# Attention output products at slots 9, 11, 13 and 14 of a tile, and a last output split into 352 and 160 columns

## The chip, the cores and the metric

The kernel runs on one core of one Trainium2 chip. The metric is the device time of one execution in microseconds (us). Before the change it is 293.71 us, the median of 6 runs, which lie between 293.46 and 293.94 us. A core has a matrix engine (TensorE, PE in the profile, with its weight loads shown as PEld), VectorE (DVE), ScalarE (ACT) and GpSimd (POOL), and SyncE (SP), which here only issues transfers. Each engine works through its own queue in order, and engines wait for each other on semaphores. PSUM is the memory that the matrix engine writes its results to; other engines copy ("evict") the results from there.

## The reference

Inputs are q, k and v, each 8 batches x 8 heads x 576 positions x 64, and the weights of a feed-forward block. Everything is float32; the kernel computes the products in bfloat16.

```
q_s = softmax of q over its last axis (64);  k_s = softmax of k over the positions (576)
kv  = einsum('bhsd,bhse->bhde', k_s, v)          # 64 x 64 for each batch and head
att = einsum('bhsd,bhde->bhse', q_s, kv)
x   = att as 4608 tokens x 512
h   = x @ w_in                                    # 4608 x 2048
g   = h + sin(alpha * h)**2 / alpha
out = g @ w_out                                   # 4608 x 512
```

## The kernel before, in words

The 4608 tokens are cut into nine tiles of 512 (t = 0 to 8). A batch of the attention has 576 tokens, nine groups of 64, so tiles and batches do not line up: batch b fills the columns 576b to 576b + 575 of `xT`, the transposed attention result (4 x 128 features by 4608 tokens), and tile t reads the columns 512t to 512t + 511 of it.

A tile is a loop over 16 *slots* (`ni`), one for each 128 of the 2048 hidden features. In slot `ni` of tile t, `mm_h` (L226, matmuls at L235) makes one 128x512 block of h with four matmuls of 512 columns; `sine` (L239) runs Sin on ACT (L241) and then the square, on ACT (L243), POOL (L245) or DVE (L247); `combine` (L250, instruction at L251) makes the bfloat16 block of g on DVE. Each h block lies in one PSUM buffer until its combine has run. There are four such buffers, taken in turn; in tile 2 slots 4, 5, 10 and 11 borrow others.

The second product, g @ w_out, runs as a stream (`o_stream`, L408, matmuls at L255): for each of the four groups of 128 tokens of a tile, 16 matmuls of 512 columns accumulate in one PSUM bank, and `evac_o` (L258) copies the bank to SBUF (L261) and writes it out with two transfers (L264). From tile 3 on the stream of tile t-1 is woven into the slots of tile t: two or three of its matmuls follow each slot's `mm_h` (L488), after 23 of them in slot 0. The third group of 128 tokens ends in slot 10, and its copy, on DVE, stands behind combine(10) in DVE's queue.

The attention of a later batch is woven in too. In tiles 3 to 6 that is batch b = t + 1; in tile 2 it is batch 3. For tiles 3 to 6: in slot 0 ACT takes the exponentials of q and k, and DVE and POOL normalise q into `qn`; in slot 4 `q_transpose_dma` (L194) asks SP for a transposing transfer of `qn` into `qT`; and `attn_back` (L451), called in slot `ni` with n = `ni` - 5, does the rest. At n = 0 (slot 5) it makes the kv products and DVE normalises them into `kbd`. Then it calls `attn_out` (L206) four times. Call number m makes feature pair m // 2 and half m % 2 of the batch's tokens: half 0 is the first 256 tokens, half 1 the other 320. A call is two matmuls (L212) of 256 or 320 columns into the two banks of a PSUM tile `xp`, and one cast (L215) that evicts both into `xT`. I name the calls xp0 to xp3 and their casts xT0 to xT3. `xp` comes from the pool `ps_a`, which has one buffer: the matmuls of a call cannot start before the cast of the call before has ended. In tiles 3 to 6 all casts are on DVE; in tile 2 they alternate between two engines, taken by the parity of n.

The order of the code is the order of each queue. In tiles 3 to 6 a slot is: `mm_h(ni)`, `attn_back`, `sine(ni)`, `combine(ni)`, the stream. So a cast in slot `ni` stands on DVE between combine(ni-1) and combine(ni). In tile 2 (L463 to L466) a slot is: `mm_h(ni)`, `sine(ni)` with its square, `combine(ni-2)`, `attn_back`. So a cast of slot `ni` stands on ACT behind Sin(ni), and behind square(ni) where `SQ2` gives that square to ACT; on DVE it stands behind combine(ni-2). Slots 9, 11 and 14 of tile 2 have the square on ACT, slots 10, 12, 13 and 15 on POOL. There is no output stream in tile 2.

Tiles 7 and 8 carry no attention. After tile 8 (L493 to L499) the output stream of that tile runs alone. Three groups of 128 tokens go as before; the last group is made in two parts of 256 columns, each with 16 matmuls (L498), a copy on DVE and two transfers of 64 tokens, one issued by SP and one by ACT.

Of the kernel before, what the change touches and what calls it, by code (L numbers as in the profile page):

```python
# [15 lines left out]
F32 = mybir.dt.float32  # L16
# [7 lines left out]
def kernel(  # L24
# [14 lines left out]
    nc = tc.nc  # L39
    ctx.enter_context(nc.allow_non_contiguous_dma(reason="layout"))  # L40
    B, H, S, D = q.shape
    dm = H * D
# [4 lines left out]
    nN = d_ff // 128  # L47
    MF = 512
    nT = NT // MF
# [19 lines left out]
    wout = singles.tile([128, nN, dm], BF16, name="wout")  # L69
# [76 lines left out]
    def kv_mm(b, ii, pool, split=False):  # L146

        if ii == 0 or split:
            A["kvp", b] = pool.tile([128, 2, 512], F32, name="kvp", tag="a")
        kvp, ke, vt = A["kvp", b], A["ke", b], vb[b % 2]  # L150
        for j in range(J):
            for e in range(2):
                r = slice(64 * e, 64 * e + 64)
                nc.tensor.matmul(kvp[:, e, ii * 130:(ii + 1) * 130],  # L154
                                 ke[r, j, ii * 128:(ii + 1) * 128],
                                 vt[r, j, ii * 130:(ii + 1) * 130],
                                 start=(j == 0), stop=(j == J - 1))

    def kv_norm(b, i0=0, i1=2):

        kt, m = kbd[b % 2], i1 - i0
        kvr = small.tile([128, 2, 2, 2], F32, name="kvr")[:, :, 0:m]
        src = A["kvp", b][:, :, i0 * 130:i1 * 130].rearrange("p e (ii x c) -> p e ii x c", ii=m, x=2)
        nc.vector.reciprocal(kvr, src[:, :, :, :, D])
        for x in range(2):
            r = slice(64 * x, 64 * x + 64)
            nc.vector.tensor_tensor(kt[r, :, i0:i1, r], src[r, :, :, x, 0:D],
                                    kvr[r, :, :, x].unsqueeze(3).to_broadcast([64, 2, m, D]), op=ALU.mult)
# [37 lines left out]
    def attn_out(b, ii, half, pool, eng):  # L206
        qT, kt = A["qT", b], kbd[b % 2]
        j0, j1 = XO[half]
        n = (j1 - j0) * P
        xp = pool.tile([128, 2, 512], F32, name="xp", tag="a")  # L210
        for e in range(2):
            nc.tensor.matmul(xp[:, e, 0:n], kt[:, e, ii], qT[:, ii, j0:j1, e * 64:(e + 1) * 64],  # L212
                             start=True, stop=True)
        c0 = (J * b + j0) * P
        eng(xT[:, 2 * ii:2 * ii + 2, c0:c0 + n], xp[:, :, 0:n])  # L215
# [8 lines left out]
    G = {}  # L224
# [29 lines left out]
    def mm_o(t, j, ni, acc):  # L254
        nc.tensor.matmul(acc, G[t][:, ni, j * 128:(j + 1) * 128], wout[:, ni, :],  # L255
                         start=(ni == 0), stop=(ni == nN - 1))

    def evac_o(t, j, acc, eng, cols=None, queues=None):  # L258
        cols = cols or slice(0, dm)
        o = opool.tile([128, dm], F32, name="o")  # L260
        eng(o[:, cols], acc)  # L261
        for hf in range(2):
            blk = t * BPT + 2 * j + hf
            (queues or (nc.sync, nc.sync))[hf].dma_start(out=out_v[blk // J, blk % J][:, cols],  # L264
                                                         in_=o[64 * hf:64 * hf + 64, cols])


    ACT_CP, DVE_CP, GP_CP = nc.scalar.copy, nc.vector.tensor_copy, nc.gpsimd.tensor_copy
# [59 lines left out]
    def h_slot(t, ni, sq, lag, wide=None):  # L328
        hp = mm_h(t, ni, wide)
        lag.append((t, ni, hp, sine(t, ni, hp, sq)))  # L330

    def flush(lag, keep):
        while len(lag) > keep:
            combine(*lag.pop(0))
# [14 lines left out]
    def take(it, n=1000):  # L349
        for _ in range(n):  # L350
            if next(it, 0) == 0:
                return
# [4 lines left out]
    with tc.tile_pool(name="ps_e", bufs=2, space=PSUM, reuse_waits="tile") as ps_e:  # L357
# [4 lines left out]
        for ni in range(nN):  # L362
            h_slot(0, ni, "PAPDPAPADPAPPDAP"[ni], lag, lent)
            flush(lag, 1)
            if ni in late:
                name, x, b, hv = late[ni]
# [37 lines left out]
    ps_o = ctx.enter_context(tc.tile_pool(name="ps_o", bufs=2, space=PSUM, reuse_waits="tile"))  # L404
    ps_a = ctx.enter_context(tc.tile_pool(name="ps_a", bufs=1, space=PSUM, reuse_waits="tile"))


    def o_stream(t, eng=DVE_CP):  # L408
        for j in range(4):
            acc = ps_o.tile([128, dm], F32, name="op", tag="o")  # L410
            for ni in range(nN):
                mm_o(t, j, ni, acc)
                if ni == nN - 1:
                    evac_o(t, j, acc, eng)
                yield
# [20 lines left out]
    c0 = J * 2 * P  # L436
# [11 lines left out]
    q_transpose_dma(3)  # L448
    load_batch(4)

    def attn_back(b, n, engs=(DVE_CP, DVE_CP)):  # L451
        if n == 0:
            kv_mm(b, 0, ps_a)
            kv_mm(b, 1, ps_a)
            kv_norm(b)
        elif 5 <= n < 9:
            attn_out(b, (n - 5) // 2, (n - 5) % 2, ps_a, engs[n % 2])

    def lent():
        return ps_o.tile([128, MF], F32, name="op", tag="o")  # L460
# [2 lines left out]
    for ni in range(nN):  # L463
        h_slot(2, ni, SQ2[ni], lag, lent)
        flush(lag, 2)
        attn_back(3, ni - 5, (DVE_CP, ACT_CP))  # L466
    flush(lag, 0)

    for t in range(3, nT):
        b = t + 1 if t + 1 < B else None  # L470
        os = o_stream(t - 1)
        done = 0
        for ni in range(nN):
            hp = mm_h(t, ni)
            if b is not None:
                if ni == 4:
                    q_transpose_dma(b)
                attn_back(b, ni - 5)
            s = sine(t, ni, hp, "A")
            combine(t, ni, hp, s)  # L480
            if b is not None and ni == 0:
                exp_q(b)
                exp_k(b)
                cast_v(b, [GP_CP, GP_CP])
                norm_q(b, [GP])
                if b + 1 < B:
                    load_batch(b + 1)
            want = 23 + 21 * ni // 8 if b is not None else 4 * (ni + 1)  # L488
            take(os, min(64, want) - done)
            done = min(64, want)  # L490
        take(os)

    take(o_stream(nT - 1), 48)  # L493
    for h in range(2):
        cols = slice(h * 256, h * 256 + 256)
        acc = ps_o.tile([128, 256], F32, name="op", tag="o")
        for ni in range(nN):
            nc.tensor.matmul(acc, G[nT - 1][:, ni, 384:512], wout[:, ni, cols], start=(ni == 0), stop=(ni == nN - 1))  # L498
        evac_o(nT - 1, 3, acc, DVE_CP, cols, (nc.sync, nc.scalar))  # L499


# [1 line left out]
_INS = ['q', 'k', 'v', 'moe_w_in', 'moe_w_out', 'moe_alpha']  # L503
_OUTS = [((4608, 512), 'float32')]
# [25 lines left out]
```

The softmax here doesn't subtract the row's maximum and nothing guards it: scores larger than these inputs give would overflow.

## Time and profile before

| | |
|---|---|
| median of 6 runs | 293.71 us |
| the profiled execution: its own time | 293.54 us |
| its span, first to last instruction | 291.8 us |
| granted clock of TensorE | 1.000 |
| PE busy | 279.1 us (96%) |
| ACT busy | 226.9 us (78%) |
| DVE busy | 188.0 us (64%) |
| POOL busy | 85.4 us (29%) |
| chain that ended last, by engine | PE 76%, DVE 9%, ACT 5%, POOL 3%, issue 3%, DMA 3% |

How to read it: the busy time of PE is a sum of modelled matmul lengths that overlap, so 96% does not say that only 4% are idle. A matmul of 512 columns has a length of 379 ns in the records, but the next one starts 216 ns after it. The distance between starts is what counts: where a matmul starts later than that after the one before it, PE waited. In timeline lines the columns are the start and the length in us, the engine, the line, the operation with its output and inputs, the count of merged instructions, and in brackets the idle time ahead of it with what ended it.

### The profile page before, as it was taken

To read this page: it belongs to the slowest core of one execution; us is meant where nothing else is said; L and a number is where in the kernel's file an instruction comes from. 1 tells how busy PE (TensorE), PEld (TensorE's weight loads), DVE (VectorE), ACT (ScalarE), POOL (GpSimd) and SP (SyncE) were. 2 spreads that over 40 slices of the span, in tenths; PEclk is the share of its full clock that TensorE was granted. 3 is DMA by queue.
4 is the path that set the end of the run, shared out by engine and by line. 5 is a ranking of instruction groups with operands and counts; after the bars stand their busy time and mean duration, and the time that the engine had idled before them with its cause. 6 is when DMAs were issued, how large, how long until landed. Compare 5 with 4: busy or idle time off the path is not lost.

```text
span 291.8 us, 4261 instructions
## 1 busy us (share of the span) xinstructions
PE 279.1 (96%) x1576; PEld 132.6 (45%) x1576; DVE 188.0 (64%) x275; ACT 226.9 (78%) x320; POOL 85.4 (29%) x78
## 2 busy tenths in 40 slices
PE   2999999999999999999999999999999999999994
PEld 1444455444454445444444454444444444444444
DVE  3758955798958657864786568756774555555412
ACT  4779946999569899789987998799977777777500
POOL 0939581566674744002600061005000000000000
PEclk9999999999999999999999999999999999999999
DMA  7999999964889975109920993113411111111143
GB/s 245 308 180 206 356 254 333 396 230 124 209 144 368 393 241 117 37 19 335 293 49 19 289 316 72 36 39 67 86 38 36 36 36 38 36 36 37 38 108 73
DMA packets 35253, 45.77 MB, mean 157 GB/s; under 512 B 15888, under 2 KB 19744, under 8 KB 35232
## 3 DMA queue, kind: packets, MB, share of 16 engines
q1 hardware_dynamic: 29632, 34.09, 40.7%
q0 software_dynamic: 5408, 11.27, 15.2%
q8 instruction: 12, 0.20, 0.3%
q10 hardware_dynamic: 192, 0.14, 0.2%
q14 instruction: 9, 0.07, 0.1%
HBM read 36.71 MB, written 9.44 MB: 158 GB/s over the span
## 4 chain that ended last, share of the span: by engine, by line
PE 76%; DVE 9%; ACT 5%; POOL 3%; issue 3%; DMA 3%; ACTq 0%
PE op L255 32%; PE hp L235 31%; PE hp L255 4%; DVE g L251 3%; PE warm L299 2%; POOL s L245 2%; DVE xT L215 2%; ACT s L241 2%; PE xp L212 2%; PE kvp L154 2%; DVE o L261 1%; DMA st_q<-in_q_dram 1%; DMA qT<-qn 1%; PE op L498 1%; PE hh L235 1%
## 5 line engine op out<-in xcount | busy, mean ns | idle before, releaser
L251 DVE SCALAR_TENSOR_TENSOR g<-s,inva_sb,hp 128x512 bf16<-128x512 f32 x130 | 95.3, 746 | 64.6 <-ACT s L243 52.1
L235 PE MATMUL hp<-xT,win 128*128 128x512 bf16 x520 | 129.5, 379 | 0.2
L255 PE MATMUL op<-wout,g 128*128 128x512 bf16 x496 | 124.0, 379 | 0.0
L241 ACT ACTIVATE s<-hp,alpha_sb 128x512 f32<-128x512 f32 x130 | 87.8, 682 | 29.4 <-PE hp L235 25.3
L235 PEld LDWEIGHTS <-win 128*128 128x128 bf16 x576 | 56.1, 98 | 68.2 <-issue 2.0
L255 PEld LDWEIGHTS <-g 128*128 128x128 bf16 x560 | 54.1, 98 | 62.7 <-issue 1.6
L243 ACT ACTIVATE s<-s 128x512 f32<-128x512 f32 x112 | 70.6, 631 | 3.6
L143 POOL TENSOR_TENSOR qn<-qe,qs 128x1152 bf16<-128x1152 bf16 x13 | 27.5, 2129 | 83.8 <-DVE qs L137 67.7
L245 POOL TENSOR_TENSOR s<-s 128x512 f32<-128x512 f32 x27 | 28.4, 1059 | 24.0 <-ACT s L241 23.7
L261 DVE COPY o<-op 128x512 f32<-128x512 f32 (+1 forms) x33 | 21.9, 665 | 10.2 <-PE op L255 7.6
L114 ACT ACTIVATE qe<-st_q 128x1152 bf16<-128x1152 f32 x16 | 18.0, 1158 | 2.8 <-DMA st_q<-in_q_dram 2.8
L114 ACT ACTIVATE ke<-st_k 128x1152 bf16<-128x1152 f32 x16 | 17.8, 1152 | 3.0 <-DMA st_k<-in_k_dram 3.0
L136 DVE TENSOR_REDUCE qs<-qe 128x36 f32<-128x2304 bf16 x5 | 12.8, 2553 | 10.8 <-ACT qe L114 10.7
L128 POOL CAST vb<-st_v 128x1152 bf16<-128x1152 f32 x14 | 16.4, 1202 | 8.2 <-DMA st_v<-in_v_dram 8.2
L215 DVE CAST xT<-xp 128x512 bf16<-128x512 f32 (+1 forms) x22 | 16.5, 753 | 2.8 <-PE xp L212 2.7
L255 PE MATMUL hp<-wout,g 128*128 128x512 bf16 x64 | 15.1, 379 | 0.4 <-DVE g L251 0.3
L212 PE MATMUL xp<-qT,kbd 128*128 128x256 bf16 (+1 forms) x56 | 10.8, 285 | 2.1 <-DVE xT L215 1.0
L154 PE MATMUL kvp<-vb,ke 64*128 64x130 bf16 x288 | 9.8, 216 | 0.5 <-ACT qT L187 0.4
L114 ACT ACT_TABLE_LOAD x7 | 9.0, 1283 | 1.3 <-PEq L514 1.2
L154 PEld LDWEIGHTS <-ke 64*128 64x128 bf16 x288 | 8.2, 93 | 3.8 <-issue 2.1
L299 PE MATMUL warm<-qe,identb 128*128 128x512 bf16 x19 | 7.5, 564 | 2.4 <-ACT qe L114 2.4
L212 PEld LDWEIGHTS <-kbd 128*128 128x128 bf16 x56 | 5.3, 97 | 9.2 <-issue 3.8
(59 smaller groups left out, 121.3 us busy)
## 6 DMA issues: line engine op xcount, KB each, us to landing
out_dram<-o SPq DMA_DIRECT2D x70, 128.0 KB, 2.4
st_q<-in_q_dram SPq DMA_DIRECT2D x5, 1152.0 KB, 6.2
st_k<-in_k_dram SPq DMA_DIRECT2D x5, 1152.0 KB, 8.6
st_v<-in_v_dram SPq DMA_DIRECT2D x5, 1152.0 KB, 10.8
st_k<-in_k_dram POOLq DMA_DIRECT2D x2, 1152.0 KB, 10.9
wout<-in_moe_w_out_dram POOLq DMA_DIRECT2D x4, 512.0 KB, 14.6
st_q<-in_q_dram SPq DMA_DIRECT2D x2, 576.0 KB, 4.5
st_k<-in_k_dram SPq DMA_DIRECT2D x2, 576.0 KB, 6.8
```

Source lines behind the costliest of these rows:

```text
L114: nc.scalar.activation(dst[:, :, ii * 128:(ii + 1) * 128].rearrange("p j (x d) -> p x j d", x=2), src[:, ii::2], AX.Exp)
L143: engs[ii % len(engs)].tensor_tensor(qn[:, ii].rearrange("p j (x d) -> p j x d", x=2), qe[:, ii], part.unsqueeze(3).to_broadcast([128, J, ...
L154: nc.tensor.matmul(kvp[:, e, ii * 130:(ii + 1) * 130], ke[r, j, ii * 128:(ii + 1) * 128], vt[r, j, ii * 130:(ii + 1) * 130], start=(j == 0 ...
L212: nc.tensor.matmul(xp[:, e, 0:n], kt[:, e, ii], qT[:, ii, j0:j1, e * 64:(e + 1) * 64], start=True, stop=True)
L215: eng(xT[:, 2 * ii:2 * ii + 2, c0:c0 + n], xp[:, :, 0:n])
L235: nc.tensor.matmul(hp, win[:, ki, ni * 128:(ni + 1) * 128], xT[:, ki, t * MF:(t + 1) * MF], start=(ki == 0), stop=(ki == 3))
L241: nc.scalar.activation(s, hp, AX.Sin, scale=alpha_sb[:, ni:ni + 1])
L243: nc.scalar.activation(s, s, AX.Square)
L245: nc.gpsimd.tensor_tensor(s, s, s, op=ALU.mult)
L251: nc.vector.scalar_tensor_tensor(G[t][:, ni], in0=s, scalar=inva_sb[:, ni:ni + 1], in1=hp, op0=ALU.mult, op1=ALU.add)
L255: nc.tensor.matmul(acc, G[t][:, ni, j * 128:(j + 1) * 128], wout[:, ni, :], start=(ni == 0), stop=(ni == nN - 1))
L261: eng(o[:, cols], acc)
```

## The change

`attn_back` gets a tuple of the four values of n at which it calls `attn_out`; the call number is now the index in the tuple, and the engine of the cast is taken by the parity of the call number, no longer by that of n. In tiles 3 to 6 the calls move from slots 10, 11, 12, 13 to slots 9, 11, 13, 14. In tile 2 they move from slots 10, 11, 12, 13 to slots 10, 12, 13, 14, and the casts, which were on ACT, DVE, ACT, DVE, are now on DVE, ACT, DVE, ACT. The last 128 tokens' output is made in parts of 352 and 160 columns in place of 256 and 256.

```diff
-    def attn_back(b, n, engs=(DVE_CP, DVE_CP)):
+    def attn_back(b, n, engs=(DVE_CP, DVE_CP), xs=(4, 6, 8, 9)):
         if n == 0:
             kv_mm(b, 0, ps_a)
             kv_mm(b, 1, ps_a)
             kv_norm(b)
-        elif 5 <= n < 9:
-            attn_out(b, (n - 5) // 2, (n - 5) % 2, ps_a, engs[n % 2])
+        elif n in xs:
+            m = xs.index(n)
+            attn_out(b, m // 2, m % 2, ps_a, engs[m % 2])
...
         h_slot(2, ni, SQ2[ni], lag, lent)
         flush(lag, 2)
-        attn_back(3, ni - 5, (DVE_CP, ACT_CP))
+        attn_back(3, ni - 5, (DVE_CP, ACT_CP), (5, 7, 8, 9))
...
     take(o_stream(nT - 1), 48)
-    for h in range(2):
-        cols = slice(h * 256, h * 256 + 256)
-        acc = ps_o.tile([128, 256], F32, name="op", tag="o")
+    for c0, c1 in ((0, 352), (352, 512)):
+        acc = ps_o.tile([128, dm], F32, name="op", tag="o")[:, 0:c1 - c0]
         for ni in range(nN):
-            nc.tensor.matmul(acc, G[nT - 1][:, ni, 384:512], wout[:, ni, cols], start=(ni == 0), stop=(ni == nN - 1))
-        evac_o(nT - 1, 3, acc, DVE_CP, cols, (nc.sync, nc.scalar))
+            nc.tensor.matmul(acc, G[nT - 1][:, ni, 384:512], wout[:, ni, c0:c1], start=(ni == 0), stop=(ni == nN - 1))
+        evac_o(nT - 1, 3, acc, DVE_CP, slice(c0, c1), (nc.sync, nc.scalar))
```

In the main loop the call `attn_back(b, ni - 5)` is unchanged and takes the new default.

## The prediction

> **What bounds the kernel now.** I read the page first, then the chain of waits, then PE, DVE and ACT by timeline around the moved calls. The chain is PE for 76% of the span of 291.8 us, at a granted clock of 1.000, so what counts is where PE starts late. In tile 3, PE's timeline has:
>
> ```profile
> 119.84 0.43 PE L212 MATMUL xp<-qT,kbd 128*128 128x320 bf16 x2
> 120.11 0.59 PE L255 MATMUL op<-wout,g 128*128 128x512 bf16 x2
> 120.54 1.03 PE L235 MATMUL hp<-xT,win 128*128 128x512 bf16 x4
> 121.83 0.38 PE L212 MATMUL xp<-qT,kbd 128*128 128x256 bf16 x2 [0.26 <-DVE xT L215]
> ```
>
> Matmuls of 512 columns start 0.216 us apart (the last line of the fence on tile 2 below: (2.75 - 0.38) / 11). The four of slot 12 start at 120.54, so xp2 could start at 120.54 + 4 x 0.216 = 121.41. It starts at 121.83: PE loses 0.42 us to the cast xT1. DVE's timeline says why that cast is late:
>
> ```profile
> 118.40 0.75 DVE L251 SCALAR_TENSOR_TENSOR g<-s,inva_sb,hp 128x512 bf16<-128x512 f32 x1 [0.76 <-ACT s L243]
> 119.06 0.69 DVE L215 CAST xT<-xp 128x512 bf16<-128x512 f32 x1
> 119.70 0.75 DVE L251 SCALAR_TENSOR_TENSOR g<-s,inva_sb,hp 128x512 bf16<-128x512 f32 x1
> 120.36 0.68 DVE L261 COPY o<-op 128x512 f32<-128x512 f32 x1
> 120.96 0.81 DVE L215 CAST xT<-xp 128x640 bf16<-128x640 f32 x1
> ```
>
> From combine(9) on, DVE has five instructions without a gap, the output copy among them, and xT1 is the last. In front of them it was idle for 0.76 us. The chain has the same cast in the other tiles:
>
> ```profile
> 151.41 0.74 DVE xT L215
> ...
> 181.78 0.74 DVE xT L215
> ```
>
> and again at 212.15. Between starts PE loses 0.42 us at each of these places. Tile 2 has a different pattern:
>
> ```profile
> 91.14 1.03 PE L235 MATMUL op<-xT,win 128*128 128x512 bf16 x4
> 92.71 0.43 PE L212 MATMUL xp<-qT,kbd 128*128 128x320 bf16 x2 [0.55 <-ACT xT L215]
> 92.98 1.03 PE L235 MATMUL hp<-xT,win 128*128 128x512 bf16 x4
> 94.06 0.38 PE L212 MATMUL xp<-qT,kbd 128*128 128x256 bf16 x2
> 94.28 1.02 PE L235 MATMUL hp<-xT,win 128*128 128x512 bf16 x4
> 95.26 0.43 PE L212 MATMUL xp<-qT,kbd 128*128 128x320 bf16 x2
> 95.53 2.75 PE L235 MATMUL hp<-xT,win 128*128 128x512 bf16 x12
> ```
>
> Counted the same way, xp1, xp2 and xp3 start 0.71, 0.21 and 0.12 us late: 1.04 us in tile 2.
>
> **Constants.** Two matmuls of 256 columns take 0.22 us of PE's queue and two of 320 take 0.27. PE's last matmul to Sin takes 0.42 (the fourth of slot 14 of tile 2 starts at 96.18, Sin at 96.59). A cast's end to PE is 0.05 (92.66 to 92.71), PE's last product to a waiting cast 0.31 (256 columns) or 0.33 (320). Sin to its square is 0.72, square to the next 0.54, Sin to the next 0.57. On DVE a combine holds the queue for 0.66, a copy for 0.60, a cast for 0.63 (512) or 0.74 (640).
>
> **Part 1, tiles 3 to 6.** In the times of tile 3. Slot 9: xp0 follows `mm_h(9)` at 116.81. xT0 runs behind combine(8) (116.89) from 117.55 to 118.24, inside the idle 0.76 us, so combine(9) stays at 118.40. This hides 0.69 us of DVE; without that gap combine(9) would only be later, which has room. PE is 0.22 later from here. Slot 10: combine(10) at 119.92, the output copy at 120.58. Slot 11: xp1 at 119.84, as before; xT1 now waits behind the copy, from 121.18 to 122.00, and combine(11), queued behind it, ends at 122.66. Nobody needs xT1 until slot 13, where xp2 is ready at 122.92: 0.87 us of room. xT2 runs from 123.65 to 124.34, behind combine(12) (122.99), and xp3 in slot 14 is ready at 124.65: 0.26 of room. `mm_h(15)` then starts at 125.35; it started at 125.77. So 0.42 a tile, -1.69 in four (0.422 each). From slot 9 on ACT waits for PE (a slot of PE takes 1.5 to 1.7 us, Sin and square 1.26), so it does not take the gain back. xT3 ends at 125.98; the next tile starts at 127.3 and reads none of xT3's columns.
>
> One call comes a slot earlier and needs `qT`. Its transfers are issued at 110.67, 141.13, 171.56 and 201.93 and land 4.6, 5.1, 5.1 and 4.6 us later; slot 9's products come at 116.8, 147.2, 177.5 and 207.9. The least room is 0.9 us; past it, each microsecond of lateness would cost PE as much in that tile. No transfer and no work of POOL or SP is moved past another; only the casts change place in DVE's queue.
>
> **Part 2, tile 2.** The casts change engines as well as slots. xp0 stays at 90.92. xT0 is now on DVE, behind combine(8), from 92.41 to 93.09. Slot 11 has no call. Slot 12: PE is ready at 92.87 and waits 0.28. xT1, 640 columns, is on ACT behind Sin(11), square(11) and Sin(12): it runs from 94.05 to 94.74 (0.69, the mean of that form on ACT). xp2 in slot 13, ready at 94.28, waits 0.51 and starts at 94.79. xT2 on DVE ends at 95.90, xp3 in slot 14 waits 0.08 and starts at 95.95. xT3 then goes to ACT at the worst place:
>
> ```profile
> 96.59 0.69 ACT L241 ACTIVATE s<-hp,alpha_sb 128x512 f32<-128x512 f32 x1 [0.57 <-PE hp L235]
> 97.31 0.63 ACT L243 ACTIVATE s<-s 128x512 f32<-128x512 f32 x1
> 97.85 1.25 ACT L241 ACTIVATE s<-hp,alpha_sb 128x512 f32<-128x512 f32 x2
> ```
>
> These are Sin(14), square(14), and Sin of slot 15 and of tile 3's slot 0. Sin(14) would start at 96.07 and the square at 96.79, so xT3 runs from 97.33 to 98.03. Tile 3's `mm_h(3, 0)` is ready at 97.08 and its third matmul, at 97.51, reads columns 1984 to 2047 of xT3: it waits until 98.08, 0.56 us. New waits: 0.28 + 0.51 + 0.08 + 0.56 = 1.43 against 1.04, so PE is 0.39 later. Queued behind xT3 on ACT are Sin(15) and Sin(3, 0); the latter comes 0.29 later (98.71, was 98.42), and with it the exponentials and the combine for which PE waits in slot 5 of tile 3, at 108.89 (0.19 us late now). PE's delay melts into that wait down to ACT's 0.29. I take +0.29. Bounds: all waits gone, -1.04; the wait for xT3 at the first matmul instead of the third, another 0.43 on 0.39, +0.82.
>
> **Part 3, the end.** Rows give 0.057 us between transposes of 128 columns, each with its own weight load (12 in 0.68), 0.109 at 256 columns, 0.135 at 320 and 0.216 at 512. On that line 160 columns take 0.070 and 352 take 0.149, together as much as twice 256: 0. The bounds for the narrow ones are 0.057 and 0.109, so -0.21 to +0.62 for 16. Against the row speaks the Trainium skill, "TensorE: Matmul & The Clock Gate", section "Back-to-back issue gap": a stream of load-and-matmul pairs is given 81 ns at 128 columns and 131 at 512. By it, 160 columns would take an estimated 85 ns, and the narrow part would be 0.24 us longer. This trace has 57 and 216, so I stay with the rows.
>
> The last copy shrinks: 0.424 for 256 columns and 0.680 for 512 make 1.0 ns a column, so 0.10 less for 160. It starts at 288.12 as before, since the PE work is equal. The two last transfers have 40 KB in place of 64; those landed 1.9 (SP) and 2.2 us (ACT) after issue, 128 KB in 2.4. Bounds 0 and (2.4 - 1.9) / 64 x 24 = 0.19 less; I take 0.05 less, near the end that the ACT row, the last to land, supports. The wider first part's copy (0.52) and issue (0.55) are over 0.3 us before the second's issue. The end: -0.15, from -0.50 to +0.52.
>
> **Sum:** -1.69 + 0.29 - 0.15 = -1.55. The profiled execution took 293.54 us (1.74 around its span), 0.17 under the median; from there 291.99, from the median of 293.71, which I use, 292.2.
>
> **Rivals.** (A) Tile 2 costs nothing, or its waits go too: 293.71 - 1.69 - 0.15 = 291.9, down to 290.8 with 1.04 more. For it: slot 11 is now free of calls. Against: ACT's queue above. (B) In tiles 3 to 6 the wait only moves to slot 14, or ACT eats the gain in the next tile: 1.69 comes back, 293.85, no change. For it: slots 13 and 14 are adjacent, with 0.26 of room. Against: xp1 in slot 11 (119.84) followed its neighbour without loss. (C) Slower: at slot 14, ACT is a whole block (1.26) behind, so combine(12) and xT2 are. Then xp3 waits 1.00, +0.58 a tile, 293.71 + 4 x 0.58 + 0.14 = 296.2. It decides from a lag of 0.65. For it: in slots 6 to 8 combines come back to back, ACT having been behind after the exponentials. Against: ACT idles 0.16 before Sin(9).
>
> **How the numbers follow.** Forecast 0.77, A 0.11, B 0.07, C 0.05. A measurement can tell about 0.2%, 0.6 us. The forecast's own range is 291.9 to 292.7: 0.3 less where tile 2 costs nothing, 0.5 more where it costs 0.82. Towards A and the end's lower bound (0.35 under 291.9) I go to 291.4, towards the end's upper bound to 293.0; B, C and most of A's lower part lie outside. Faster by over 0.2%: 0.88 (forecast and A); within: 0.07 (B); slower: 0.05 (C).
>
> **What would show it.** Right: no late xp2 in slot 13 of tiles 3 to 6; xT0 between combine(8) and combine(9); in tile 2 a wait of about 0.5 us before xp2 and another inside `mm_h(3, 0)`, both on ACT's cast; a last copy of 0.32 us. Wrong: PE waiting on xT2 in slot 14, on `qT` in slot 9, or longer at slots 4 and 5 of each next tile.

## The result, and the profile after

The changed kernel takes 291.92 us (median of 19 runs, 291.58 to 293.14), beside 293.93 us for the kernel before (42 runs). The ratio is 0.9938, with a 95% interval of 0.9929 to 0.9947: 1.8 us less, between 1.6 and 2.1 (the two medians differ by 2.0, the means of the same runs by 1.8). The profiled execution took 291.62 us with a span of 289.8 us, 1.9 us under that of before. The forecast was 1.55 us less and 292.2 us.

PE's timeline in tile 3, from the call in slot 11 to the call in slot 13:

```profile
119.82 0.43 PE L212 MATMUL xp<-qT,kbd 128*128 128x320 bf16 x2
120.09 0.59 PE L255 MATMUL op<-wout,g 128*128 128x512 bf16 x2
120.52 1.03 PE L235 MATMUL hp<-xT,win 128*128 128x512 bf16 x4
121.38 0.81 PE L255 MATMUL op<-wout,g 128*128 128x512 bf16 x3
122.03 1.03 PE L235 MATMUL hp<-xT,win 128*128 128x512 bf16 x4
122.89 0.38 PE L212 MATMUL xp<-qT,kbd 128*128 128x256 bf16 x2
```

Each start follows from the one before by the count times 0.216 us (0.135 for xp1): no late start is left. The profile before had xp2 0.42 us late here. DVE's timeline around the same slots:

```profile
117.53 0.68 DVE L215 CAST xT<-xp 128x512 bf16<-128x512 f32 x1
118.38 0.75 DVE L251 SCALAR_TENSOR_TENSOR g<-s,inva_sb,hp 128x512 bf16<-128x512 f32 x1 [0.16 <-ACT s L243]
119.89 0.75 DVE L251 SCALAR_TENSOR_TENSOR g<-s,inva_sb,hp 128x512 bf16<-128x512 f32 x1 [0.76 <-ACT s L243]
120.55 0.68 DVE L261 COPY o<-op 128x512 f32<-128x512 f32 x1
121.15 0.81 DVE L215 CAST xT<-xp 128x640 bf16<-128x640 f32 x1
```

xT0 has gone into the idle time ahead of combine(9) (0.76 us before, 0.16 now). xT1 still stands behind the output copy and ends at 121.96, even later than before (121.77). It no longer matters, since xp2 is first ready at 122.89.

Tile 2 got worse, as forecast. PE's timeline there:

```profile
92.88 0.43 PE L212 MATMUL xp<-qT,kbd 128*128 128x320 bf16 x2
93.15 1.02 PE L235 MATMUL hp<-xT,win 128*128 128x512 bf16 x4
94.50 0.38 PE L212 MATMUL xp<-qT,kbd 128*128 128x256 bf16 x2 [0.32 <-ACT xT L215]
94.72 1.02 PE L235 MATMUL hp<-xT,win 128*128 128x512 bf16 x4
95.66 0.43 PE L212 MATMUL xp<-qT,kbd 128*128 128x320 bf16 x2
95.93 1.46 PE L235 MATMUL hp<-xT,win 128*128 128x512 bf16 x6
97.76 0.59 PE L235 MATMUL hp<-xT,win 128*128 128x512 bf16 x2 [0.37 <-ACT xT L215]
```

The line at 95.93 holds six matmuls of 0.216, so the next should start at 97.23; it starts at 97.76. It is the third matmul of `mm_h(3, 0)`, and it waits for xT3 on ACT. Counted from starts, the waits are 0.28, 0.49, 0.08 and 0.54 us, 1.38 in sum, against 1.04 before. ACT's timeline shows xT3 behind Sin(14) and its square:

```profile
95.78 0.69 ACT L241 ACTIVATE s<-hp,alpha_sb 128x512 f32<-128x512 f32 x1 [0.74 <-PE hp L235]
96.50 0.63 ACT L243 ACTIVATE s<-s 128x512 f32<-128x512 f32 x1
97.04 0.67 ACT L215 CAST xT<-xp 128x640 bf16<-128x640 f32 x1
97.61 1.47 ACT L241 ACTIVATE s<-hp,alpha_sb 128x512 f32<-128x512 f32 x2
```

At the end, DVE's timeline has the two copies of 352 and 160 columns; the last was 0.42 us long with 256:

```profile
285.31 0.53 DVE L261 COPY o<-op 128x352 f32<-128x352 f32 x1 [1.69 <-PE op L499]
286.42 0.33 DVE L261 COPY o<-op 128x160 f32<-128x160 f32 x1 [0.58 <-PE op L499]
```

To compare traces I use the time from the first kv matmul of tile 2 to the end of the span, because what lies ahead of it differs between executions of code that is the same: that matmul starts at 85.47 us in the profile before, at 85.20 after, and anywhere from 85.24 to 85.96 in the runs below. From there to the end it is 206.29 us before and 204.63 after: 1.66 us less. The other 0.26 us of the difference between the two spans lie ahead of everything that the change touches.

### The profile page after: what moved, and what is told of

It is laid out like the page before. It is cut to its first block, busy times and chain, and to the rows that moved or that the text cites. A ratio compares the mean times of both kernels' runs of the same rounds, so it can differ in the third digit from the quotient of the medians.

```text
span 289.8 us, 4261 instructions
## 1 busy us (share of the span) xinstructions
PE 277.8 (96%) x1576; PEld 131.9 (46%) x1576; DVE 187.7 (65%) x275; ACT 227.4 (78%) x320; POOL 85.2 (29%) x78
## 4 chain that ended last, share of the span: by engine, by line
PE 83%; DVE 5%; DMA 4%; POOL 2%; ACT 2%; issue 2%; SPq 1%; ACTq 0%
PE hp L235 35%; PE op L255 34%; PE hp L255 4%; DMA st_v<-in_v_dram 3%; PE kvp L154 2%; PE xp L212 2%; DVE g L251 2%; DMA qT<-qn 1%; PE op L499 1%; PE op L235 1%; PE hh L235 1%; POOL s L245 1%; DVE qs L141 1%; ACT s L241 1%; SPq L91 1%
## 5 line engine op out<-in xcount | busy, mean ns | idle before, releaser
L261 DVE COPY o<-op 128x512 f32<-128x512 f32 (+2 forms) x33 | 21.9, 665 | 10.3 <-PE op L255 7.9
L141 DVE TENSOR_REDUCE qs<-qe 128x18 f32<-128x1152 bf16 x6 | 7.9, 1322 | 2.7 <-ACT qe L114 2.7
L299 PE MATMUL warm<-qe,identb 128*128 128x512 bf16 x19 | 6.6, 505 | 3.0 <-ACT qe L114 3.0
```

## The experiments

Each kernel is the kernel before with the edit shown, unless said otherwise. Where an edit gives `attn_back` a tuple `xs`, its body is that of the changed kernel with `engs[m]` in place of `engs[m % 2]`: the engines of the casts are given call by call. The default of `xs` holds for tiles 3 to 6, the call `attn_back(3, ...)` is that of tile 2.

### Only tiles 3 to 6

```diff
-    def attn_back(b, n, engs=(DVE_CP, DVE_CP)):
+    def attn_back(b, n, engs=(DVE_CP,) * 4, xs=(4, 6, 8, 9)):
...
-        attn_back(3, ni - 5, (DVE_CP, ACT_CP))
+        attn_back(3, ni - 5, (ACT_CP, DVE_CP, ACT_CP, DVE_CP), (5, 6, 7, 8))
```

> Only tiles 3 to 6 get the new slots (9, 11, 13, 14); tile 2 and the end are as before. Theory (the late cast xT1, last of five instructions in a row on DVE, was the whole loss there, 0.42 us a tile): -1.69 us, about 0.58% faster; PE has no late start from slot 9 to the next tile, and DVE is idle before combine(10). Rival (the wait moves to slot 14, or ACT returns the gain in slots 4 and 5 of the next tile): 0 us. Rival (the change gains elsewhere, in tile 2 or at the end): less than 1 us.

Measured: 292.24 against 293.89 us, ratio 0.9941 (0.9923 to 0.9960). From tile 2's kv matmul to the end it is 204.56 us, 1.73 less than before, and no late start is left in slots 9 to 15 of tiles 3 to 6. From one tile's kv matmuls to the next tile's it is 29.94 us where it was 30.37, three times over, so nothing is given back in slots 4 and 5. The theory holds; the wait did not move.

### Only tile 2

```diff
-    def attn_back(b, n, engs=(DVE_CP, DVE_CP)):
+    def attn_back(b, n, engs=(DVE_CP,) * 4, xs=(5, 6, 7, 8)):
...
-        attn_back(3, ni - 5, (DVE_CP, ACT_CP))
+        attn_back(3, ni - 5, (DVE_CP, ACT_CP, DVE_CP, ACT_CP), (5, 7, 8, 9))
```

> Only tile 2 is changed: slots 10, 12, 13, 14 and casts on DVE, ACT, DVE, ACT. Theory (two casts of 640 columns behind Sin and square on ACT cost more than the waits removed): waits of 0.28, 0.5, 0.08 and 0.55 us on PE against 0.71, 0.21 and 0.12 before, part of it taken up by the wait in slot 5 of tile 3: +0.25 us, 0.1% slower. Rival A (a free slot 11 helps): -0.3 to -1.0 us.

Measured: 294.05 against 293.89 us, ratio 0.9999 (0.9986 to 1.0013), too small for the times to show. The trace shows it: PE waits 0.28, 0.49, 0.08 and 0.53 us, as in the changed kernel, the wait in slot 5 of tile 3 shrinks from 0.19 to 0.10, and the stretch to the end is 206.49 us, 0.20 longer than before. From the kv matmuls of tile 2 to those of tile 3 it is 24.62 us against 24.38.

### Only the end

```diff
-    for h in range(2):
-        cols = slice(h * 256, h * 256 + 256)
+    for c0, c1 in ((0, 352), (352, 512)):
...
```

> Only the last group of 128 tokens is split into 352 and 160 columns. Theory: PE work equal (0.149 and 0.069 us between starts), a copy 0.10 us shorter and transfers that land 0.05 to 0.10 us sooner: -0.2 us, 0.07%, which a comparison of times can hardly tell. Rival (weight loads bound the narrow matmuls at 0.085 us or more): +0.1 us or worse, seen as starts more than 0.08 us apart.

Measured: 293.95 against 293.89 us, ratio 0.9998 (0.9985 to 1.0011). In the trace the stretch to the end is 206.03 us, 0.26 less. The starts are 0.149 us apart at 352 columns and 0.069 at 160, as the line through the rows of the trace before has them, so PE's work is equal. The last copy is 0.10 us shorter, and the time from the issue of the last transfers to SyncE's last wait for them went from 2.22 to 2.12 us. That shorter landing repeats: with 64 KB the eight traces have 1.93 to 1.95 us from issue to landing on SP and 2.19 to 2.21 on ACT, with 40 KB the three traces have 1.83 to 1.84 and 2.10 to 2.11.

### Only the third and the fourth call, one slot later

```diff
-    def attn_back(b, n, engs=(DVE_CP, DVE_CP)):
+    def attn_back(b, n, engs=(DVE_CP,) * 4, xs=(5, 6, 8, 9)):
...
-        attn_back(3, ni - 5, (DVE_CP, ACT_CP))
+        attn_back(3, ni - 5, (ACT_CP, DVE_CP, ACT_CP, DVE_CP), (5, 6, 7, 8))
```

> Tiles 3 to 6 have their calls at slots 10, 11, 13, 14: only the third and the fourth call move, one slot later; tile 2 and the end are as before. Theory (all that matters is that the third call does not follow directly on the cast that stands behind the output copy): xT1 ends at the same time as before, xp2 in slot 13 finds it done, and all of the 0.42 us a tile is gained: -1.69 us, 0.58% faster, as with all four calls. Rival (the earlier first call, which fills DVE's idle time before combine(9), is what gains): 0 us, PE still waits 0.3 us or more before xp2 or xp3.

Measured: 292.19 against 293.89 us, ratio 0.9941 (0.9921 to 0.9961); 204.57 us to the end, 1.72 less. This equals the run with all four calls moved. PE's timeline of tile 3 from xp1 in slot 11 on:

```profile
120.20 0.44 PE L212 MATMUL xp<-qT,kbd 128*128 128x320 bf16 x2
120.48 0.60 PE L255 MATMUL op<-wout,g 128*128 128x512 bf16 x2
120.91 1.03 PE L235 MATMUL hp<-xT,win 128*128 128x512 bf16 x4
121.77 0.81 PE L255 MATMUL op<-wout,g 128*128 128x512 bf16 x3
122.42 1.03 PE L235 MATMUL hp<-xT,win 128*128 128x512 bf16 x4
123.28 0.38 PE L212 MATMUL xp<-qT,kbd 128*128 128x256 bf16 x2
```

xp1 comes after slot 11's h matmuls as before, and xp2, one slot later, starts on time (this trace runs 0.37 us later than the profile before throughout). The earlier first call, which the forecast described first, is worth nothing here.

### Only the first call, one slot earlier

```diff
-    def attn_back(b, n, engs=(DVE_CP, DVE_CP)):
+    def attn_back(b, n, engs=(DVE_CP,) * 4, xs=(4, 6, 7, 8)):
...
-        attn_back(3, ni - 5, (DVE_CP, ACT_CP))
+        attn_back(3, ni - 5, (ACT_CP, DVE_CP, ACT_CP, DVE_CP), (5, 6, 7, 8))
```

> Tiles 3 to 6 have their calls at slots 9, 11, 12, 13: the first call moves one slot earlier, the other three stay; tile 2 and the end are as before. Theory (only the third call's distance from the cast behind the output copy matters): xT1 now ends at about 121.97 in tile 3's old times, 0.2 us later than before, since the copy in front of it is later by the first call's 0.22 us of PE; xp2, still in slot 12, is ready at 121.41 and waits about 0.6 us in place of 0.42: +0.2 us a tile, +0.8 us in all, 0.26% slower. Rival (the early first call is what gains): -0.8 to -1.7 us.

Measured: 294.72 against 293.70 us, ratio 1.0035 (1.0022 to 1.0048): slower. The stretch to the end is 207.10 us, 0.80 longer than before. PE's timeline of tile 3:

```profile
120.75 1.03 PE L235 MATMUL hp<-xT,win 128*128 128x512 bf16 x4
122.25 0.38 PE L212 MATMUL xp<-qT,kbd 128*128 128x256 bf16 x2 [0.47 <-DVE xT L215]
```

xp2 could start at 120.75 + 0.86 = 121.61 and is 0.64 us late, 0.22 more than before in each of four tiles. The extra 0.22 us is the first call's own time on PE. It now lies ahead of slot 10's h matmuls, so Sin(10), its square, combine(10), the output copy and xT1 all come later by it; ahead of xp2 there is as much work on PE as before. DVE's timeline has the three (this trace runs 0.21 us later than the profile before ahead of the move):

```profile
120.12 0.75 DVE L251 SCALAR_TENSOR_TENSOR g<-s,inva_sb,hp 128x512 bf16<-128x512 f32 x1 [0.77 <-ACT s L243]
120.78 0.68 DVE L261 COPY o<-op 128x512 f32<-128x512 f32 x1
121.38 0.81 DVE L215 CAST xT<-xp 128x640 bf16<-128x640 f32 x1
```

DVE idles before combine(10) and waits for ACT: taking xT0 out of the way there does not bring combine(10) forward. It could not, as ACT's timeline of the profile before shows with the square of slot 10:

```profile
119.03 0.63 ACT L243 ACTIVATE s<-s 128x512 f32<-128x512 f32 x1
```

This square ended at 119.66, and combine(10) started at 119.70. So this move, taken alone, costs time; the later third and fourth call are all of the gain.

### The output copy out of DVE's queue

```diff
-                    evac_o(t, j, acc, eng)
+                    evac_o(t, j, acc, ACT_CP if j == 2 and 2 <= t <= 5 else eng)
```

> The kernel before, with all calls and the end where they were; only the copy of the third group of 128 tokens in tiles 3 to 6, which stands in DVE's queue in front of xT1, is on ACT. Theory (that copy makes xT1 late): xT1 starts 0.6 us earlier, xp2 in slot 12 does not wait, ACT has room for the copy, and 0.42 us a tile is gained: -1.7 us, 0.58% faster. Rival (xT1 is late because of the combines alone, or ACT, now with the copy, is late for the next square): less than 0.8 us is gained.

Measured: 292.37 against 294.02 us, ratio 0.9944 (0.9923 to 0.9964). DVE's timeline of tile 3 goes from combine(10) straight to xT1:

```profile
119.75 0.75 DVE L251 SCALAR_TENSOR_TENSOR g<-s,inva_sb,hp 128x512 bf16<-128x512 f32 x1
120.42 0.82 DVE L215 CAST xT<-xp 128x640 bf16<-128x640 f32 x1
```

and PE's timeline has xp2 directly behind the h matmuls of slot 12, all calls being in their old slots:

```profile
120.60 1.03 PE L235 MATMUL hp<-xT,win 128*128 128x512 bf16 x4
121.47 0.38 PE L212 MATMUL xp<-qT,kbd 128*128 128x256 bf16 x2
```

Each of the four late starts is gone, and from one tile's kv matmuls to the next it is again 29.94 us. xT1 starts 0.60 us earlier against its surroundings (120.42 where it was 120.96, in a trace that runs 0.06 us later). The copy in front of xT1 was the cause. On ACT it costs nothing there: it starts at 119.62 and the next Sin at 120.10, where in the profile before it started at 120.04, and PE's matmuls of slot 12 are 0.06 later in this trace too (120.60 against 120.54).

### Tile 2: slots alone and engines alone

```diff
-    def attn_back(b, n, engs=(DVE_CP, DVE_CP)):
+    def attn_back(b, n, engs=(DVE_CP,) * 4, xs=(5, 6, 7, 8)):
... slots alone:
-        attn_back(3, ni - 5, (DVE_CP, ACT_CP))
+        attn_back(3, ni - 5, (ACT_CP, DVE_CP, ACT_CP, DVE_CP), (5, 7, 8, 9))
... engines alone:
-        attn_back(3, ni - 5, (DVE_CP, ACT_CP))
+        attn_back(3, ni - 5, (DVE_CP, ACT_CP, DVE_CP, ACT_CP), (5, 6, 7, 8))
```

> Only tile 2 is changed, and only its slots (10, 12, 13, 14); the casts stay on ACT, DVE, ACT, DVE. Theory (the swap of the engines is what made tile 2 worse): no wait before xp1 and none inside tile 3's first slot, one of about 0.9 us before xp2, behind combine(10); in sum 0.2 us better than before, and 0.4 better than with the swap. Rival (the late last call is what made it worse): again a wait in tile 3's first slot and +0.2 us.

> Only tile 2 is changed, and only the engines of its casts (DVE, ACT, DVE, ACT); its slots stay 10, 11, 12, 13. Theory (the swap makes tile 2 worse whatever the slots): xp1 waits about 1.1 us for xT0, which is now behind combine(8) on DVE, xp2 and xp3 under 0.1 us each; in sum +0.25 us against before. Rival (only the late last call hurts): waits of 1.0 us or less in sum, no loss.

Measured, slots alone: 293.74 against 293.70 us, ratio 0.9993 (0.9977 to 1.0009); the stretch to the end is 206.01 us, 0.28 less than before. One wait is left, before xp2:

```profile
94.92 0.38 PE L212 MATMUL xp<-qT,kbd 128*128 128x256 bf16 x2 [0.70 <-DVE xT L215]
```

By starts it is 0.87 us. Engines alone: 294.13 us in one run. From the kv matmuls of tile 2 to those of tile 3 it is 24.64 us against 24.38, with waits of 1.14, 0.08 and 0.08 us. PE's timeline shows the first:

```profile
93.51 0.43 PE L212 MATMUL xp<-qT,kbd 128*128 128x320 bf16 x2 [0.98 <-DVE xT L215]
```

So the new slots gain about 0.27 us in tile 2 (24.12 against 24.38 by the same measure) and the swap of the engines costs 0.25 in the old slots and 0.50 in the new ones (24.62 against 24.12). The late last call is harmless when its cast is on DVE; it hurts with the cast behind a square on ACT.

### Tile 2 with slots and engines chosen from its queues

The edit is to the changed kernel.

```diff
-    def attn_back(b, n, engs=(DVE_CP, DVE_CP), xs=(4, 6, 8, 9)):
+    def attn_back(b, n, engs=(DVE_CP,) * 4, xs=(4, 6, 8, 9)):
...
-        attn_back(3, ni - 5, (DVE_CP, ACT_CP), (5, 7, 8, 9))
+        attn_back(3, ni - 5, (DVE_CP, DVE_CP, ACT_CP, DVE_CP), (4, 6, 8, 9))
```

> The changed kernel, but with tile 2's calls also at slots 9, 11, 13, 14 and its casts on DVE, DVE, ACT, DVE, so that no cast stands behind a square on ACT. Theory: waits in tile 2 of about 0.15, 0.08 and 0.24 us, none in tile 3's first slot, so tile 2 is 0.8 us better than in the changed kernel: 0.25% faster than it, 0.85% faster than before (291.4 where before takes 293.9). Rival (tile 2 is bound by ACT's own work, 16 Sin and 6 squares, not by the casts): the waits move to ACT's combines and at most 0.2 us is gained over the changed kernel.

Measured: 291.38 against 293.70 us, ratio 0.9914 (0.9896 to 0.9931). The stretch to the end is 203.74 us, 0.89 less than in the changed kernel and 2.55 less than before. PE's timeline in tile 2:

```profile
92.64 0.43 PE L212 MATMUL xp<-qT,kbd 128*128 128x320 bf16 x2
92.91 1.89 PE L235 MATMUL hp<-xT,win 128*128 128x512 bf16 x8
94.69 0.38 PE L212 MATMUL xp<-qT,kbd 128*128 128x256 bf16 x2
94.91 1.02 PE L235 MATMUL hp<-xT,win 128*128 128x512 bf16 x4
96.05 0.43 PE L212 MATMUL xp<-qT,kbd 128*128 128x320 bf16 x2
96.32 1.89 PE L235 MATMUL hp<-xT,win 128*128 128x512 bf16 x8
```

The waits by starts are 0.15, 0.05 and 0.29 us, and the eight matmuls at 96.32, which reach into tile 3's first slot, run without a break. By the traces this version beats both kernels. By the times it beats the kernel before; it did not run beside the changed kernel, and the two ratios to the kernel before (0.9896 to 0.9931 here, 0.9929 to 0.9947 there) just touch.

### The end in 448 and 64 columns

```diff
-    for h in range(2):
-        cols = slice(h * 256, h * 256 + 256)
+    for c0, c1 in ((0, 448), (448, 512)):
...
```

> Only the last group of 128 tokens is split, into 448 and 64 columns. It measures what bounds narrow matmuls with a weight load each. Theory of the line through the rows (57 ns at 128 columns, 69 at 160, 109 at 256): 0.19 us between starts at 448 columns and 0.03 at 64. Rival (weight loads bound): the 64-column matmuls start 0.055 us or more apart, 0.4 us more in sum. Either way the first part's copy of about 0.62 us now stands in front of the second's, which was not so with 160 columns.

Measured: 294.22 us in one run. PE's timeline has the last of the wide matmuls and the sixteen narrow ones in one line:

```profile
287.55 0.82 PE L498 MATMUL op<-wout,g 128*128 128x448 bf16 x17
```

The wide one takes 0.189 to the next start and the last narrow one has a length of 0.193, which leaves 0.44 us for 15 distances: 0.029 us each, on the line through the wider rows, with a new 128x128 weight load for each. Weight loads do not bind even there. The end is nevertheless later: the stretch is 206.66 us, 0.63 more than with 352 and 160. The two copies, 448 and 64 columns, now follow each other on DVE:

```profile
287.94 0.76 DVE L261 COPY o<-op 128x448 f32<-128x448 f32 x2 [2.33 <-PE op L498]
288.59 1.11 SPq L264 DMA_DIRECT2D out_dram<-o  x2
288.59 1.38 ACTq L264 DMA_DIRECT2D out_dram<-o  x2
```

The second copy ends at 288.69, but SP issues its transfer only at 289.15 and ACT at 289.24, behind those of the first part (issued at 288.59). In the profile before, an issue follows the end of its copy by 0.03 us; by that they would have been issued at an estimated 288.72, 0.43 and 0.52 us sooner. Counted from the first matmul of the last group, ACT's last issue is 0.48 us later than with 352 and 160 columns, and it takes 2.22 us to land where that took 2.10: together nearly all of the 0.63.

## Why the prediction was right, point by point

- **Part 1, tiles 3 to 6: forecast -1.69 us, measured -1.73 alone.** xT0, the output copy, xT1 and xT2 start within 0.03 us of the forecast's times in the changed kernel's trace, and the next tile returns nothing. What the forecast did not separate is which move pays: it is that of the third and the fourth call, which were tried together, and the wait that went is the third call's. The first call's move, which it placed with care in DVE's idle time, costs 0.2 us a tile when it is made alone. The five instructions in a row that the forecast blames overstate the cause: combine(10) waited for its square until 119.66 anyway and started at 119.70, so combine(9) and xT0 ahead of it cost nothing. What made xT1 late is the output copy behind combine(10), as the run with that copy on ACT shows.
- **`qT` in slot 9.** No product of slot 9 waits in the trace after. The least room there is 0.8 us (landed at 175.92, used at 176.69), near the 0.9 forecast.
- **Part 2, tile 2: forecast +0.29 us, measured +0.20 alone to the end, +0.24 from the kv matmuls of tile 2 to those of tile 3.** The second stretch holds all that the part touches. The four waits were forecast as 0.28, 0.51, 0.08 and 0.56 us and are 0.28, 0.49, 0.08 and 0.54. The wide cast on ACT took 0.67 and 0.68 us instead of the 0.69 taken from the mean row. That PE's delay melts into the wait in slot 5 of tile 3 was right as well: that wait shrank from 0.19 to 0.10.
- **Part 3, the end: forecast -0.15 us, measured -0.26 alone.** PE's work and the copy were as forecast. The term that was too small is that of the transfers: 0.05 was taken and the traces show 0.10 for the landing. Copy and landing make 0.20; of the other 0.06, 0.04 lie ahead of the last group, in code that this run leaves as it was, and 0.02 behind SyncE's last wait. The figure of the Trainium skill that spoke against the narrow part, 81 ns at 128 columns ("TensorE: Matmul & The Clock Gate", "Back-to-back issue gap"), does not hold here: 69 ns at 160 columns and 29 at 64.
- **The sum.** The parts alone give -1.73 + 0.20 - 0.26 = -1.79, the changed kernel's trace -1.66, the forecast -1.55, the times -1.8 (1.6 to 2.1). Of the 0.13 us between the parts and the whole, 0.07 lie where the part in question changes nothing: in the traces of tile 2 alone and of the end alone, an untouched tile takes 30.36 us where the trace before has 30.37. Another 0.02 lie behind SyncE's last wait and count in two of the three parts. Differences of a few hundredths between such long stretches of two traces are therefore no evidence; the waits and distances at the place itself are.
- **The rivals.** A is out: tile 2 costs time. B and C are out: xp3 in slot 14 does not wait, and ACT waits for PE before each Sin of slots 9 to 15.

## What to carry to other kernels

Here PE's wait for an eviction went when the next user of the buffer was moved away from it, or when what stood in front of the cast was taken out of its queue; both gave the same 0.42 us a tile, while an earlier first call alone made it worse. Before calling a row of instructions on an engine the cause, ask for each of them when its own inputs were ready. When an engine assignment follows from an index, a new index can swap it unasked: read each queue behind which the moved instruction now stands, slot by slot, as tile 2 shows with 0.25 to 0.50 us. Where every wait in a stretch could be put down to a line, as here, starts and distances read from one trace were enough to work out the next arrangement's waits to within a tenth of a microsecond.

## What the runs showed of the hardware

At a granted clock of 1.000, matmuls with a 128x128 weight load each kept the line of about 0.42 ns a column from 512 columns (0.216 us) down to 64 (0.029 us), though each weight load has a length of 98 ns in the records. Narrowing the last part stops paying for another reason: at 64 columns the issue of the first part's transfers (0.47 us on SP, 0.55 on ACT) stands in front of the second's.
